# One last-row item of four transposed by the tensor engine instead of by VectorE and DRAM, with its product joined to its neighbour's

## The chip, the cores and the metric

The kernel runs on one core of one Trainium2 chip. The metric is the device time of one launch in microseconds (us); lower is better. The kernel before takes 1477.64 us (median of 3 runs, 1477.17 to 1479.41).

In the profile PE is the tensor engine's matmul, PEld its weight load, DVE is VectorE, ACT is ScalarE, POOL is GpSimd and SP is SyncE, which here only issues transfers (SPq is its queue). L727 is line 727 of the kernel before; a name such as `o` or `pt` is a tile.

## The reference

Attention that keeps the 32 largest scores of each row, then a layer with an exact GELU. All of it is float32.

```python
# q, k, v: (8, 8, 576, 64)
scores = np.matmul(q, k.transpose(0, 1, 3, 2)) / np.sqrt(64)
kth = np.partition(scores, -32, axis=-1)[..., -32:-31]
scores = np.where(scores >= kth, scores, -1e9)
attn = np.exp(scores - scores.max(-1, keepdims=True))
attn = attn / (attn.sum(-1, keepdims=True) + 1e-09)
x = np.matmul(attn, v)            # then (B, S, H*D): 4608 rows of 512
h = x @ w_in                      # 512 -> 2048
g = 0.5 * h * (1.0 + erf(h / np.sqrt(2)))
out = g @ w_out                   # 2048 -> 512
```

## The kernel before

**Items.** The attention is cut into 144 items of 128 rows of probabilities by twice 576 keys. A batch has eight heads, taken as four pairs, and 576 rows, that is four blocks of 128 and a last block of 64. An item of the first kind is one block of one pair, its two heads side by side. An item of the second kind, a last-row item, takes the 64 last rows of two pairs, that is of four heads. So a batch has 16 items of the first kind and 2 of the second. Batches go in twos, a ring of `RINGS` = 36 items: the even batch ends with its two last-row items (places 16 and 17 of the ring) and the odd batch starts with its own (places 18 and 19). These are the four last-row items of the title. There are four rings; in the first one these items are handled like the others, so the change bears on three: items 52 to 55, 88 to 91 and 124 to 127.

**Steps.** The kernel's order is written out by hand: a loop over steps n, each of which issues work of several items to all engines, in an order that every engine then keeps. In step n the scores of items n+2 and n+3 are multiplied (`scores`, at even n), DVE finds the 32 largest of item n (`top_k`), ACT makes the mask and the exponential of item n-1 (`softmax`), POOL sums, small statistics and the division (`threshold`, L516 and L517; `add_small`, L529; `normalise`, L571), and the probabilities of item n-2 are transposed. Between these, pieces of the layer with GELU (`mlp`: `h_ps`, `y_ps`, `seven`) are set, so that PE has work while the attention waits for the others.

**Two ways to transpose.** The product with v needs the probabilities transposed, in the tile `pt`, of which there is one buffer with room for two items (an even and an odd one). The odd items of the first kind, and everything up to item 26, go through PE: `transposes` gives one transpose of the tails (L647, together with the last keys' scores of item n+2, L371) and eight of 128 by 128 (L661); ACT copies them to `pt` (L650, L676). Items for which `squared` is true go another way: DVE transposes them in squares of 32 (`square_p`, L595, inside `top_k` of step n), SP writes them to DRAM in four transfers (`write_p`, L605, end of step n) and reads them back into `pt` in four (`read_p`, L615, in the next step). Even items of the first kind (but one per ring) and all last-row items behind item 26 are squared; the latter are called `delayed`.

**Products.** `attend(i)` multiplies with v into a PSUM tile `o` from `bank`, and ACT copies `o` to `xT` (L732, or L744 for a last-row item) when `copy_x` is called. From step 13 on `bank` has one buffer only, so that the next tile from it (`t_ps` or `tp_t` of L371, `seven`, `o`) waits until the copy before is done. For items of the first kind the product comes with the odd item. For last-row items: item 52 has its product at the start of step 56 (`even_last`), item 53 late in step 57, item 54 early and item 55 late in step 59 (`mid`, `mids`). The late ones are copied on ACT behind the first half of the softmax of item n-1. The same holds for 88 to 91 and 124 to 127, with 36 and 72 added.

**SP's queue.** SP issues in program order, and each issue waits for what it needs. Besides the writes and reads above it has the loads of q, k and v and the stores of y. When a last-row product of an even batch is done, the next batch's v is loaded for its two pairs, four transfers a pair (L138, L142). `issue` puts a load off to `flush`, behind the step's write, when the step has one (`held`); `issue_soon` runs those of `soon`, behind the step's read. Stores of y are collected and issued by `run_stores` at the end of the following step.

Of the kernel before, what the change touches and what calls it, by code (L numbers as in the profile page):

```python
# [14 lines left out]
def kernel(  # L15
# [78 lines left out]
            return raws[n][pair % 2 if pair < SQUARES else 0]  # L94
        return raws[n][pair % len(raws[n])]

    held, late_issues, soon = [False], [], []

    def issue_soon():
        while soon:  # L100
# [9 lines left out]
    def flush():  # L110
        held[0] = False
        while late_issues:
            late_issues.pop(0)()

    def load(n, pair, queue=None, queue2=None):
        if pair >= n_pairs:
# [161 lines left out]
    def bank(name):  # L278

        tag = "z" if few[0] else ("z", "y0", "y1", "y2")[turn[0] % 4]  # L280
        turn[0] += 1
        return ps.tile([P, 512], f32, tag=tag, bufs=1, name=name)
# [292 lines left out]
    def squared(i):  # L575

        if not SINGLE.stop - 2 < i < N - 2:
            return False
        return items[i][1] == NM or (i % 2 == 0 and i % RINGS != 12)

    def delayed(i):

# [117 lines left out]

    copies = []

    def column(tok):

        at = tok % RING
        return at if at < COLS else at - COLS

    def attend(i):

        if i < 0 or i >= N:  # L710
            return False
        pair, t = items[i]
        b, at = divmod(pair, NP)
        if t < NM and t % 2 == 0:
            return False
        pt = pt_now[0]
        o = bank("o")
        n, row = (2 * P, (t - 1) * P) if t < NM else (TL, SM)
        tok = place_of(b, row)
        gap = RING if t == NM else COLS if tok % RING >= COLS else RING - COLS  # L720
        assert read[0] >= tok - gap + n
        c = slice(column(tok), column(tok) + n)
        if t < NM:
            vt = raw_of("v", pair)
            for j in range(NJ):
                for e in range(2):
                    nc.tensor.matmul(  # L727
                        o[e * D : (e + 1) * D, 0:n], lhsT=vt[:, j, e, :],
                        rhs=pt[:, e * NJ + j if j < NM else NM, :],
                        start=(j == 0), stop=(j == NJ - 1),  # L730
                    )
            copies.append(lambda: nc.scalar.copy(out=xT[:, at, c], in_=o[:, 0:n]))  # L732
        else:
            for r in range(2):
                vt = raw_of("v", pair + r)
                for j in range(NJ):
                    for e in range(2):
                        nc.tensor.matmul(
                            o[e * D : (e + 1) * D, r * TL : (r + 1) * TL],
                            lhsT=vt[:, j, e, :],  # L740
                            rhs=pt[:, e * NJ + j if j < NM else NM, i % 2 * P :][:, half(r, e)],
                            start=(j == 0), stop=(j == NJ - 1),
                        )
            copies.append(lambda: nc.scalar.copy(  # L744
                out=xT[:, at : at + 2, c],
                in_=o[:, 0 : 2 * TL].rearrange("p (r n) -> p r n", n=TL),
            ))

        if t == (NM if b % 2 == 0 else NM - 1):
            for r in range(2 if t == NM else 1):  # L750
                f = lambda r=r: load("v", pair + r + NP)
                if r == 0 and delayed(i):
                    soon.append(f)
                else:
                    issue(f)
        if at == (NP - 1 if t < NM else NP - 2):
            assert n_tok[0] == tok
            n_tok[0] = tok + n
        return True
# [414 lines left out]
    for n in range(ahead):  # L1174

        held[0] = n < N and squared(n - 2)
        mid = [i for i in (n - 5, n - 4) if delayed(i) and n % 2 and (i % 2 or i in starts)]
        even_last = delayed(n - 4) and n % 2 == 0 and n - 4 not in starts
        if not mid and not even_last:
            read_p(n - 3)  # L1180

        def mids():
            attend(mid.pop(0))
            if not mid:
                copy_x()
                read_p(n - 3)
                issue_soon()
        left[0] = room_in(n)
        few[0] = n > START + 2
        eager[0] = n > N  # L1190
        left[0] += closes(n - 3) - closes(n - 2)
        if not waits(unit_in(n)):
            weights_add(unit_in(n))
        if n > 0:
            larger(n + 1)
        for piece in squares_in.pop(n, []):
            piece()
        if n == 1:

            for e in range(2):  # L1200
                select(0, e)
            for e in range(2):
                softmax(0, e)
        two = few[0] and n % 2 == 0 and n + 3 < N and items[n + 3][1] < NM
        scores(n + 2, two)
        if two:
            scores(n + 3)
        if even_last:
            product = attend(n - 4)
            issue_soon()  # L1210
            read_p(n - 3)
        else:
            product = not delayed(n - 3) and attend(n - 3)
        if len(mid) == 2:
            mids()
        late = n > START
        if n != 1 and n < START:

            for e in range(2):
                select(n - 1, e)  # L1220
            softmax(n - 1, 0)
        copy_x()
        if n == START:

            for e in range(2):
                select(n - 1, e)
            softmax(n - 1, 0)
        if waits(unit_in(n)):
            weights_size(unit_in(n))
            weights_add(unit_in(n))  # L1230
        mlp(1)
        if closes(n - 3):
            ready[0] = n_tok[0]
        if few[0] and n % 2:
            run_gelus()
        tr = transposes(n - 2)
        if product and n > START and done[0] < len(pieces) and pieces[done[0]][0] > ready[0]:

            for piece in tr[:1]:
                piece(n + 2 if few[0] else None)  # L1240
            tr, ready[0] = tr[1:], n_tok[0]
        if not few[0] and n > START:
            softmax(n - 1, 0)
        mlp(1)
        if n != 1 and not late:
            softmax(n - 1, 1)
        if few[0]:
            softmax(n - 1, 0)
            if n % 2:
                mlp(ODD)  # L1250
                if mid:
                    mids()
        mlp(1)
        prep = prep_in.pop(n, [])
        if n == 0:
            weights_size(unit_in(1))
            keep_busy(14, ident)
        if n == START + 1:

            for piece in prep:  # L1260
                piece(None)
            prep = []
        if len(prep) > 1 and len(tr) == 3:
            tr, prep = tr[:1] + prep[:1] + tr[1:], prep[1:]
        now = tr[:-1]
        if few[0]:
            now, tr, prep = tr + prep[:1], [], prep[1:]
        for x, piece in enumerate(now):
            piece(n + 2 if few[0] else None)
            ready[0] = n_tok[0]  # L1270
            if few[0] and x == 2:
                break
            mlp(1)
        ready[0] = n_tok[0]
        if late:
            softmax(n - 1, 1)
        if n > 0:
            smaller(n + 1)
        add_small(n - 1)
        for piece in tr[-1:] + prep:  # L1280
            piece(None)
            mlp(1)
        if n < START:

            keep_busy(4 if n == 0 else 8 if product else 14 if n < 5 else 18, ident)

        run_gelus()
        mlp(left[0])
        run_gelus()
        if n < N:  # L1290
            top_k(n, lambda: inverse(n - 1), lambda: square_p(n - 2))
            write_p(n - 2)
            flush()
            if n == 0:
                larger(1)
        else:
            inverse(n - 1)
        threshold(n)
        if n == 0:
            smaller(1)  # L1300
        normalise(n - 1)
        sum_up(n + 2)
        if n in sums_in:
            weight_sums(sums_in[n])
        run_small(6)

        if n > 0 and not waits(unit_in(n + 1)):
            weights_size(unit_in(n + 1))
        run_stores()
        if n == N:  # L1310
            run_stores()
        for m in (n + 1, n + 2):

            if m > 2 and waits(unit_in(m)) == (m == n + 1):
                load_weights(m)
        if n < NP:
            load("v", n)
        if n == 5:
            nc.vector.memset(flat["k"][0][TL:, 0:TL], 0.0)
            load("q", SQUARES)  # L1320
            load("k", SQUARES)
# [38 lines left out]
```

## Time and profile before

| | |
|---|---|
| runs | 1477.17, 1477.64, 1479.41 us |
| profiled execution, its own time | 1479.29 us |
| its span | 1477.5 us |
| PE busy | 98% of the span |
| DVE, POOL, ACT busy | 89%, 77%, 73% |
| mean granted clock of PE | 0.999 |
| transfers of `turned` and `pt` | 240 each way, 144 KB each |

The page shows one execution. Its busy shares are means over the whole kernel; a few microseconds have to be looked for in the waits of one engine and in the timelines of a stretch, which list instructions in the order of time: start, duration, engine, line, operation and tiles, how many were merged into the row, and in brackets the idle time before it and what ended it. A duration of PE has the time until the result is there, so that rows overlap; the time that an instruction takes from the next one is read from start to start.

### The profile page before, as it was taken

What the parts mean: (1) busy time and instruction counts of PE and PEld (TensorE: products, weight loads), DVE (VectorE), ACT (ScalarE), POOL (GpSimd) and SP (SyncE); (2) the same over time, 40 slices, a digit from 0 to 9 for tenths busy, and PEclk for the clock granted to TensorE, in tenths of its full rate; (3) what the DMA queues carried; (4) which work ended last, traced back from release to release, by engine and by line L of the source; (5) the groups of instructions that cost most, each with busy time, mean ns of one, the idle gap of its engine ahead of it and who ended that gap; (6) DMA issues with size and microseconds to landing.
All of it is one profiled execution on the core that took longest, in us unless ns stands there. A gap on an engine that the chain in (4) does not pass through costs nothing. (4 is left out here: it accounts for less than half of the span.)

```text
span 1477.5 us, 26521 instructions
## 1 busy us (share of the span) xinstructions
PE 1449.7 (98%) x8693; PEld 1134.6 (77%) x8693; DVE 1307.8 (89%) x3331; ACT 1082.8 (73%) x1902; POOL 1142.0 (77%) x1290
## 2 busy tenths in 40 slices
PE   8999999999999998999999999999999999999999
PEld 6776677887777776888777777787777777787787
DVE  7999899999999999899999999899999999898701
ACT  7999877877777686777777777677777777677620
POOL 6877567878898888777898978787788888887632
PEclk9999999999999999999999999999999999999999
DMA  7425210045435356345534347344543435523300
GB/s 198 144 86 129 78 47 1 24 92 103 93 71 91 67 107 129 65 95 112 102 81 78 74 74 151 76 92 96 99 101 73 89 63 97 125 61 73 68 15 15
DMA packets 544713, 127.04 MB, mean 86 GB/s; under 512 B 466464, under 2 KB 536128, under 8 KB 544576
## 3 DMA queue, kind: packets, MB, share of 16 engines
q1 hardware_dynamic: 543312, 124.93, 39.8%
q8 instruction: 69, 1.13, 0.3%
q14 instruction: 68, 0.56, 0.1%
q10 hardware_dynamic: 1200, 0.39, 0.1%
q0 software_dynamic: 64, 0.03, 0.0%
HBM read 80.47 MB, written 44.83 MB: 85 GB/s over the span
## 5 line engine op out<-in xcount | busy, mean ns | idle before, releaser
L790 PE MATMUL h_ps<-xT,w_in_sb 128*128 128x256 f32 (+1 forms) x2560 | 534.1, 361 | 0.0
L790 PEld LDWEIGHTS h_ps<-xT,w_in_sb 128*128 128x128 f32 x2560 | 437.5, 190 | 73.3 <-issue 25.2
L502 DVE MAX8 top<-lists 128x8 f32<-128x576 f32 (+1 forms) x792 | 475.5, 639 | 0.0
L505 DVE MATCH_REPLACE8 lists<-top,lists 128x288 f32<-128x288 f32 (+1 forms) x528 | 307.6, 588 | 0.0
L571 POOL TENSOR_TENSOR s<-s,stat 128x1152 f32<-128x1152 f32 x135 | 286.1, 2119 | 0.3 <-DVE stat L523 0.3
L536 ACT ACTIVATE s<-s,stat 128x576 f32<-128x576 f32 x288 | 224.7, 788 | 16.6 <-POOL stat L516 16.4
L548 ACT ACTIVATE s<-s,stat 128x576 f32<-128x576 f32 x288 | 224.6, 782 | 11.3 <-POOL lists L466 0.7
L529 POOL TENSOR_SCALAR stat<-stat 128x2 f32<-128x2 f32 x144 | 31.6, 219 | 210.4 <-ACT s L548 183.8
L474 POOL TENSOR_TENSOR lists<-lists 128x576 int32<-128x576 int32 x132 | 186.4, 1412 | 4.0
L466 POOL TENSOR_TENSOR lists<-s 128x576 int32<-128x576 int32 x133 | 188.0, 1413 | 0.0
L727 PE MATMUL o<-pt,raw_v 128*64 128x256 f32 x1280 | 152.9, 384 | 4.3 <-DMA pt<-turned 2.4
L806 ACT ACTIVATE g<-h_ps 128x512 f32<-128x512 f32 x144 | 78.2, 594 | 107.0 <-PE h_ps L790 106.8
L727 PEld LDWEIGHTS o<-pt,raw_v 128*64 128x64 f32 x1280 | 87.9, 136 | 88.3 <-issue 43.1
L946 PE MATMUL y_ps<-w_out_sb,sum 128*128 128x256 f32 x472 | 140.8, 380 | 0.0
L414 ACT ACTIVATE s<-s_ps 128x1024 f32<-128x1024 f32 x127 | 124.9, 1031 | 9.2 <-PE s_ps L406 8.8
L406 PE MATMUL s_ps<-kt,qm 64*128 64x512 f32 x512 | 129.4, 618 | 0.8 <-ACT s L412 0.8
L676 ACT COPY pt<-tp 128x1024 f32<-128x1024 f32 x73 | 74.4, 1019 | 56.2 <-PE tp L661 56.1
L505 DVE MATCH_REPLACE8 lists<-first,lists 128x288 f32<-128x288 f32 x264 | 114.2, 438 | 0.0
L946 PE MATMUL y_ps<-w_out_sb,g 128*128 128x256 f32 x480 | 113.4, 379 | 0.0
L523 DVE RECIPROCAL stat<-stat 128x2 f32<-128x2 f32 x144 | 22.9, 159 | 95.2 <-POOL stat L529 94.4
L502 DVE MAX8 first<-lists 128x8 f32<-128x288 f32 x268 | 106.5, 436 | 0.0
L441 DVE TENSOR_TENSOR lists<-s 128x576 f32<-128x576 f32 x133 | 101.1, 760 | 0.0
(162 smaller groups left out, 2483.3 us busy)
## 6 DMA issues: line engine op xcount, KB each, us to landing
turned<-s SPq DMA_DIRECT2D x240, 144.0 KB, 3.5
pt<-turned SPq DMA_DIRECT2D x240, 144.0 KB, 3.2
raw_v<-in_v_dram SPq DMA_DIRECT2D x64, 128.0 KB, 3.0
raw_q<-in_q_dram SPq DMA_DIRECT2D x112, 72.0 KB, 2.3
raw_k<-in_k_dram SPq DMA_DIRECT2D x112, 72.0 KB, 2.4
out_dram<-y SPq DMA_DIRECT2D x30, 256.0 KB, 2.1
w_out_sb<-in_moe_w_in_dram SPq DMA_DIRECT2D x14, 511.8 KB, 4.8
w_out_sb<-in_moe_w_out_dram SPq DMA_DIRECT2D x10, 511.8 KB, 4.1
```

Source lines behind the costliest of these rows:

```text
L406: nc.tensor.matmul(s_ps[:, e], lhsT=q_t[rows, :], rhs=kt[rows, main_keys(pair)], start=True, stop=True)
L414: nc.scalar.activation(spread(s, S + TL, SM), s_ps, func=AF.Copy, scale=scale)
L466: nc.gpsimd.tensor_tensor(t[:, :, 1].bitcast(i32), a.bitcast(i32), b.bitcast(i32), op=ALU.add)
L474: nc.gpsimd.tensor_tensor(into_of(i)[:, :, 1].bitcast(i32), both, top, op=ALU.subtract)
L502: nc.vector.max(x[:, e], src[:, e])
L505: nc.vector.match_replace(dst[:, e], x[:, e], src[:, e], LOWEST)
L536: nc.scalar.activation(s, s, func=AF.Prelu, bias=st["neg"][:, e : e + 1], scale=1.0, alpha=STEEP)
L548: nc.scalar.activation(s, s, func=AF.Exp, bias=st["bias"][:, e : e + 1], scale=1.0, accum_out=st["den"][:, e : e + 1],)
L571: nc.gpsimd.tensor_tensor(s, s, wide, op=ALU.mult)
L727: nc.tensor.matmul(o[e * D : (e + 1) * D, 0:n], lhsT=vt[:, j, e, :], rhs=pt[:, e * NJ + j if j < NM else NM, :], start=(j == 0), stop=(j = ...
L790: nc.tensor.matmul(h_tile(u)[:, i, :], lhsT=w_in_sb[:, ko, f * P : (f + 1) * P], rhs=xT[:, ko, c0 : c0 + n], start=(ko == 0), stop=(ko == ...
L946: nc.tensor.matmul(acc[names][:, k], lhsT=lhsT, rhs=rhs, start=(j == 0 and k == 0), stop=(j == FT // 2 - 1 and k == 1),)
```

## The change

In each of the three rings the second last-row item (53, 89, 125; place 17) is no longer squared. PE transposes it in step 55 and ACT copies it to `pt`, beside item 52's half, which is read from DRAM as before. Both products are then made in step 56, one right behind the other, in the two halves of one tile `o`, and one copy takes both to `xT`. The step that used to read item 53 and to multiply it does not do so any more. The loads of v that hang on these products are ordered anew: the first two pairs' right behind the joint product, the third's behind item 54's write, the fourth's behind item 55's write. The two stores of y that stood at the end of step 57 stand behind item 55's read at the start of step 58.

```diff
-    held, late_issues, soon = [False], [], []
+    held, late_issues, soon, later = [False], [], [], []
...
     def flush():
         held[0] = False
         while late_issues:
             late_issues.pop(0)()
+        late_issues.extend(later)
+        later.clear()
...
     def squared(i):
         if not SINGLE.stop - 2 < i < N - 2:
             return False
-        return items[i][1] == NM or (i % 2 == 0 and i % RINGS != 12)
+        if items[i][1] == NM:
+            return i % RINGS != RINGS // 2 - 1
+        return i % 2 == 0 and i % RINGS != 12
...
+    shared = []
...
     def attend(i):
...
-        o = bank("o")
+        both = t == NM and delayed(i - 1) and not delayed(i)
+        alone = t < NM or not delayed(i) or delayed(i ^ 1)
+        o = shared.pop() if both else bank("o")
+        off = 2 * TL if both else 0
...
-                            o[e * D : (e + 1) * D, r * TL : (r + 1) * TL],
+                            o[e * D : (e + 1) * D, off + r * TL : off + (r + 1) * TL],
...
-            copies.append(lambda: nc.scalar.copy(
-                out=xT[:, at : at + 2, c],
-                in_=o[:, 0 : 2 * TL].rearrange("p (r n) -> p r n", n=TL),
-            ))
+            if not alone:
+                shared.append(o)
+            else:
+                first = 0 if both else at
+                copies.append(lambda: nc.scalar.copy(
+                    out=xT[:, first : at + 2, c],
+                    in_=o[:, 0 : off + 2 * TL].rearrange("p (r n) -> p r n", n=TL),
+                ))
...
                 f = lambda r=r: load("v", pair + r + NP)
-                if r == 0 and delayed(i):
-                    soon.append(f)
+                if delayed(i):
+                    soon.insert(0, f)
+                elif both and r:
+                    later.append(f)
                 else:
                     issue(f)
...
+        def stores_later(m):
+            return m % 2 == 0 and delayed(m - 3) and m - 4 in starts
+
         even_last = delayed(n - 4) and n % 2 == 0 and n - 4 not in starts
-        if not mid and not even_last:
+        if not mid:
             read_p(n - 3)
+        if stores_later(n):
+            run_stores()
...
         if even_last:
             product = attend(n - 4)
+            attend(n - 3)
             issue_soon()
-            read_p(n - 3)
...
-        run_stores()
+        if not stores_later(n + 1):
+            run_stores()
```

## The prediction

> **What bounds the kernel now.** I read the page first, then the waits of the tensor engine (PE), then the timelines of each engine around the place that the change touches.
>
> ```profile
> span 1477.5 us, 26521 instructions
> ...
> PE 1449.7 (98%) x8693; PEld 1134.6 (77%) x8693; DVE 1307.8 (89%) x3331; ACT 1082.8 (73%) x1902; POOL 1142.0 (77%) x1290
> ```
>
> PE is idle for 27.8 us of 1477.5 only: the kernel is as long as PE's work plus its few waits. So an instruction added to PE costs its time in full, and a gain must come out of those 27.8 us. The waits of PE, longest first:
>
> ```profile
> PE o L738 <- DMA pt<-turned: 5.7, 3, 2.2
> ...
> PE o L727 <- DMA pt<-turned: 2.4, 2, 1.9
> PE t_ps L371 <- ACT xT L744: 2.2, 3, 0.7
> ```
>
> These 10.3 us all lie around the last-row items, in three places: items 52 to 55, 88 to 91 and 124 to 127 (rings 1, 2, 3 below). Ring 1 on PE, time of start and duration first, idle time and its releaser in brackets:
>
> ```profile
> 559.19 0.49 PE L371 MATMUL t_ps<-kt,qm 128*128 128x128 f32 x2 [0.74 <-ACT xT L744]
> ...
> 576.82 1.39 PE L738 MATMUL o<-pt,raw_v 128*64 128x64 f32 x40 [1.21 <-DMA pt<-turned]
> ...
> 579.41 0.49 PE L371 MATMUL tp_t<-kt,qm 128*128 128x128 f32 x2
> ...
> 587.31 2.38 PE L727 MATMUL o<-pt,raw_v 128*64 128x256 f32 x20 [1.91 <-DMA pt<-turned]
> ```
>
> 559.19 (step 57) stands behind item 53's product: the next user of that PSUM bank waits for its copy (0.74). 576.82 is item 55's product (step 59), late by its transposed rows. 587.31 (step 60) waits for item 56's. Rings 2 and 3:
>
> ```profile
> 926.13 1.39 PE L738 MATMUL o<-pt,raw_v 128*64 128x64 f32 x40 [2.25 <-DMA pt<-turned]
> ...
> 928.41 0.38 PE L371 MATMUL tp_t<-kt,qm 128*128 128x128 f32 x2
> 928.63 0.27 PE L647 MATMUL tp_t<-ident,s 128*128 128x128 f32 x1
> 928.74 0.60 PE L946 MATMUL y_ps<-w_sum,sum 128*128 128x256 f32 x2
> ...
> 929.61 1.04 PE L661 MATMUL tp<-ident,s 128*128 128x128 f32 x8
> 930.48 0.60 PE L946 MATMUL y_ps<-w_sum,g 128*128 128x256 f32 x2
> ...
> 934.81 2.38 PE L727 MATMUL o<-pt,raw_v 128*64 128x256 f32 x20 [0.52 <-DMA pt<-turned]
> ```
>
> ```profile
> 1273.51 2.12 PE L738 MATMUL o<-pt,raw_v 128*64 128x64 f32 x40 [2.20 <-DMA pt<-turned]
> ...
> 1277.37 0.39 PE L371 MATMUL tp_t<-kt,qm 128*128 128x128 f32 x2
> ...
> 1283.18 2.38 PE L727 MATMUL o<-pt,raw_v 128*64 128x256 f32 x20
> ```
>
> Ring 3 ran slower behind its wait: from product to L371 it took 3.86 us (1273.51 to 1277.37) against 2.28 in ring 2. In the first 2.1 us of it the granted clock, which stands behind the five engines' busy times, was 0.59:
>
> ```profile
> 1273.50:1275.60 2.10, 2.09 (x41) 1.98 (x41) 2.10 (x8) 1.39 (x3) 2.02 (x3) 0.59 0.93 143
> ```
>
> These 1.58 us belong to this execution: the profiled run took 1479.29 us, and without them 1477.71, which is the median shown (1477.64).
>
> **Added to PE.** Per ring, one tail transpose and eight more. From row to next row, L647 takes 0.11 us (928.63 to 928.74), the eight L661 0.87 (929.61 to 930.48): 0.98, on the path, 2.9 us in three rings. Merging two products into one run saves about two changes of tile shape, 0.1 us each at most; I count them as nothing.
>
> **Added to ACT, taken from DVE.** The two copies' groups, with busy time and mean ns:
>
> ```profile
> L676 ACT COPY pt<-tp 128x1024 f32<-128x1024 f32 x73 | 74.4, 1019 | 56.2 <-PE tp L661 56.1
> ...
> L650 ACT COPY pt<-tp_t 128x128 f32<-128x128 f32 x84 | 22.8, 271 | 3.0 <-PE tp_t L647 2.9
> ```
>
> ACT gets 1.02 + 0.27 = 1.29 us in step 55; the merge saves it one small copy in step 57, which I count as nothing. Behind the copies on ACT stands the exponential of item 54, and behind that POOL's small L529. What covers it:
>
> ```profile
> 543.85 0.22 POOL L529 TENSOR_SCALAR stat<-stat 128x2 f32<-128x2 f32 x1 [2.12 <-ACT s L548]
> 545.35 0.79 POOL L516 TENSOR_SCALAR stat<-top 128x2 f32<-128x2 f32 x1 [1.28 <-DMA turned<-s]
> ```
>
> Between L529 and L516 POOL idles 1.28 us. The row names a transfer, but L516 reads what DVE's top-k of item 55 leaves, so that is the real end, and from it the change takes a transpose of 1.36 us. So ACT's 1.1 to 1.3 us fill the gap that DVE leaves, and POOL goes on where it did, or 0.2 us earlier. I take 0.2; the bounds are 0 (ACT takes all) and 0.4. Without that cover each ring would lose up to 1.29 us.
>
> **Removed: the transfers.** Per ring four writes and four reads of SP vanish (item 53's), v's loads of the first two pairs go together behind the merged product, and the two stores of y step behind item 55's read. DVE's transposes of items 55 and 56 and SP in ring 1, then item 56's write and read in ring 2:
>
> ```profile
> 559.60 1.36 DVE L595 STREAM_TRANSPOSE s<-s 128x1152 f32<-128x1152 f32 x1
> ...
> 569.86 1.36 DVE L595 STREAM_TRANSPOSE s<-s 128x1152 f32<-128x1152 f32 x1
> ```
>
> ```profile
> 545.48 0.44 SPq L138 DMA_DIRECT2D raw_v<-in_v_dram  x1
> ...
> 548.41 2.57 SPq L615 DMA_DIRECT2D pt<-turned  x4
> ...
> 563.76 3.27 SPq L605 DMA_DIRECT2D turned<-s  x4
> ...
> 570.39 1.00 SPq L861 DMA_DIRECT2D out_dram<-y  x2
> 571.48 2.60 SPq L615 DMA_DIRECT2D pt<-turned  x4
> 574.19 3.39 SPq L605 DMA_DIRECT2D turned<-s  x4
> 581.88 2.54 SPq L615 DMA_DIRECT2D pt<-turned  x4
> ```
>
> ```profile
> 923.54 3.49 SPq L605 DMA_DIRECT2D turned<-s  x4
> ...
> 929.61 2.54 SPq L615 DMA_DIRECT2D pt<-turned  x4
> ```
>
> The rows from 563.76 on are item 55's write, the stores, 55's read, 56's write and read. A pair of v takes 2.9 us (545.48 to 548.41), a write 3.3, a read 2.6; from a write to the read that needs it 6.1 us (ring 2) to 7.7 (ring 1). With the change v's two pairs run from about 546.5 (1 us later than now, for PE's transposes) to 552.4, 54's write to 555.7, one more pair to 558.6, 54's read starts at 558.6 to 560.1. So 55's write starts between 561.2 (DVE done at 560.96) and 562.7 instead of 563.76, its read 6.1 to 7.7 later, 567.3 to 570.4, instead of 571.48. From that read to PE's product it was 5.3 us (to 576.82), so the rows are there at 572.6 to 575.7; PE comes at 576.82 - 1.21, or 0.2 later with what follows: 575.8. The DMA wait is gone. 56's write then starts between 571.3 (DVE done at 571.2) and 574.1, now 574.19, and its product is free to start that much earlier than 587.31: between 584.4 and 587.2. I take 585.4. In rings 2 and 3, with the 6.1, it is well clear.
>
> **Where the stall goes.** Both DMA waits and the L371 wait gone, less the transposes, would be 3.86 - 0.98 in ring 1 (and PE would be 0.98 - 0.74 = 0.2 late at item 55's product, as used above). But in step 59 a second thing ends just behind the DMA: the copy of item 55's product, which stands on ACT behind the first half of item 58's softmax:
>
> ```profile
> 576.20 0.78 ACT L536 ACTIVATE s<-s,stat 128x576 f32<-128x576 f32 x1 [1.24 <-POOL stat L516]
> ...
> 579.11 0.25 ACT L744 COPY xT<-o 128x128 f32<-128x128 f32 x1
> ```
>
> ```profile
> 924.47 0.77 ACT L536 ACTIVATE s<-s,stat 128x576 f32<-128x576 f32 x1 [1.24 <-POOL stat L516]
> ```
>
> ```profile
> 1271.90 0.78 ACT L536 ACTIVATE s<-s,stat 128x576 f32<-128x576 f32 x1 [1.25 <-POOL stat L516]
> ```
>
> L536 waits for item 58's threshold, that is for DVE and POOL, not for PE. From L536 the copy comes at +2.91 and L371, which needs the bank, at +3.21 (576.20 to 579.41). PE, early by then, is there at 575.8 + 2.28 = 578.1 and will stand at L371 for about 1.1 us. So L371 starts at L536 + 3.21 less the 0.2: 579.21, 927.48 and 1274.91, against 579.41, 928.41 and 1277.37. From L371 to L727 is 5.81 us without a wait (ring 3), 5.9 behind a stall (0.49 for 0.38 above), so PE is at L727 at 585.1, 933.4, 1280.8; with the transfer ring 1 starts at 585.4. That is 1.9, 1.4 and 2.4 us earlier. Behind L727 the rings ran alike whatever stood before, so it stays. PE's 2.9 us lie within the new wait and are paid already.
>
> **Sum.** 5.7 us off the profiled run: 1479.29 - 5.7 = 1473.6. To the median: ring 3's 1.58 us of low clock are mostly not in it; ring 3's gain then is 0.8, or 1.3 if a wait like ring 2's 0.52 stands there instead. 1477.64 - (1.9 + 1.4 + 0.8 to 1.3) = 1473.0 to 1473.5. I say 1473.2.
>
> One rule is weighed here. The row: after 2.20 us of waiting the clock fell to 0.59 and cost 1.58 us, while after 2.25, 1.91 and 1.21 us it cost nothing. The Trainium skill (TensorE: Matmul & The Clock Gate, Part 1) has the clock fall only after an idle window of about 3.4 us; by that rule a 1.1 us wait is free, and the sum stands. The trace disagrees once in four.
>
> **The rivals.**
> PE is held by nothing (0.15): POOL's chain comes over 1.1 us earlier since DVE has less to do, and L371 doesn't wait. Then ring 1 gains 3.86 - 0.98 = 2.9, ring 2 0.74 + 2.25 + 0.52 - 0.98 = 2.5, ring 3 at least 2.0: 1470.2. Against it: POOL's L529 at 543.85 waits for ACT, which gets later.
> The clock falls behind the new waits (0.13): up to 1.58 us a ring; one drop gives 1474.8, two 1476.4.
> The transfers stay late (0.11): v's loads in one run hold 54's write, and what L371 gains is waited away at L727 in all rings: 1476.5 to 1477.6.
> ACT becomes the bound (0.08), the slower case. In step 55 its big copy would wait for PE's transposes, as it does in step 59:
>
> ```profile
> 581.78 1.01 ACT L676 COPY pt<-tp 128x1024 f32<-128x1024 f32 x1 [1.18 <-PE tp L661]
> ```
>
> Then 1.29 + 1.18 = 2.47 us go into item 54's exponential, and if POOL's gap at 545.35 doesn't take them (its end being something else than DVE's top-k), L536 of step 59 comes 2.47 later. L727 then starts at 576.20 + 2.47 + 3.21 + 5.9 = 587.8 in ring 1, 0.5 late; in ring 2 at 936.1, 1.2 late; in ring 3, against 1281.6 without the low clock, at 1283.5, 1.9 late: 1477.64 + 3.6 = 1481.2. It turns to a loss once the delay passes about 1.3 us. Against it: ACT lies behind PE in step 55 (no idle before its copies there), so the transposes should be ready when it comes.
> The order doesn't change as said (0.01): 1477.6.
>
> **How the numbers follow.** The forecast has 0.52, with a range of its own of 1471.7 to 1475.1 (cover 0 to 0.4 in each ring, ring 1's transfer from 584.4 to 587.2). 0.2% is 2.95 us, about what a measurement of this kernel can tell: faster is below 1474.7. From the forecast 0.48, from the free PE 0.15, from the clock 0.07: faster 0.70. Same: 0.04, 0.06, 0.11 and 0.01, 0.22. Slower 0.08. The range for 8 in 10, from the free PE to the late transfers' better end: 1469.6 to 1476.6.
>
> **What would show it.** Right: no wait for pt's DMA at L738 and L727 in rings 1 to 3; a wait of L371 for xT's copy in step 59, 0.6 to 1.8 us in each ring; POOL's L516 of step 55 within 0.4 us of its old place after the row before; DVE's transposes 57 instead of 60; L661 24 more. Wrong: L371 in step 59 without a wait (then faster than said), L676 in step 55 behind a PE wait, or DMA waits of pt left at L727.

## The result, and the profile after

The changed kernel takes 1473.85 us (median of 8 runs, 1473.37 to 1474.59), the kernel before beside it 1478.04 us (8 runs, 1477.17 to 1479.56): a ratio of 0.997 with a 95% interval of 0.9959 to 0.9981, 4.2 us or 0.28% faster. The prediction was 1473.2 us, and 0.2% as the bound of what can be told.

| | before | after |
|---|---|---|
| profiled execution, its own time | 1479.29 us | 1473.45 us |
| its span | 1477.5 us | 1471.4 us |
| ring 1: start of item 56's product (L727, now L736) | 587.31 | 585.04 |
| ring 2 | 934.81 | 931.05 |
| ring 3 | 1283.18 | 1277.07 |

The lines have moved: L371 is L373 now, L516 L518, L529 L531, L536 L538, L595 L599, L605 L609, L615 L619, L647 L651, L650 L654, L661 L665, L676 L680, L727 L736, L738 L747, L744 L757, L861 L876.

The busy time of each engine on the page of the changed kernel:

```profile
PE 1450.0 (99%) x8720; PEld 1136.2 (77%) x8720; DVE 1304.3 (89%) x3328; ACT 1084.8 (74%) x1905; POOL 1141.0 (78%) x1290
```

PE has as much to do as before (1449.7), in a span that is 6.1 us shorter. What went is waiting. The longest of PE's waits after, in total, number and longest one:

```profile
PE tp_t L373 <- ACT xT L757: 4.7, 3, 1.6
```

No wait for a transfer of `pt` is left. Instead of 10.3 us in three kinds there are 4.7 in one, the one that was foretold. Ring 1 on PE after, with start, duration, and in brackets the idle time before:

```profile
539.86 0.38 PE L373 MATMUL tp_t<-kt,qm 128*128 128x128 f32 x2
540.08 0.27 PE L651 MATMUL tp_t<-ident,s 128*128 128x128 f32 x1
540.19 0.60 PE L961 MATMUL y_ps<-w_sum,sum 128*128 128x256 f32 x2
...
541.05 1.04 PE L665 MATMUL tp<-ident,s 128*128 128x128 f32 x8
541.93 0.60 PE L961 MATMUL y_ps<-w_sum,g 128*128 128x256 f32 x2
...
545.67 2.55 PE L747 MATMUL o<-pt,raw_v 128*64 128x64 f32 x80
548.15 2.86 PE L805 MATMUL h_ps<-xT,w_in_sb 128*128 128x256 f32 x12
...
575.09 1.39 PE L747 MATMUL o<-pt,raw_v 128*64 128x64 f32 x40
...
579.13 0.49 PE L373 MATMUL tp_t<-kt,qm 128*128 128x128 f32 x2 [1.59 <-ACT xT L757]
...
585.04 2.38 PE L736 MATMUL o<-pt,raw_v 128*64 128x256 f32 x20
```

The added transposes are there, L651 and eight L665; the joint product is one run of 80 (545.67); item 55's product (575.09) and item 56's (585.04) wait for nothing. Only L373 waits, for the copy of item 55's product. In rings 2 and 3 it is the same:

```profile
925.14 0.49 PE L373 MATMUL tp_t<-kt,qm 128*128 128x128 f32 x2 [1.57 <-ACT xT L757]
...
1271.16 0.49 PE L373 MATMUL tp_t<-kt,qm 128*128 128x128 f32 x2 [1.57 <-ACT xT L757]
```

The three waits are equal within 0.02 us, which transfers never were (2.25, 2.20, 1.21 before). What a ring gains itself is what its L736 is earlier by, less what the rings ahead had gained: 587.31 - 585.04 = 2.27 in ring 1, of which 0.08 was there at its start (539.94 against 539.86); 3.76 in ring 2 less the 2.33 that its own step 55 comes earlier by, 1.43; 6.11 less 3.72 in ring 3, 2.39.

### The profile page after: what moved, and what is told of

Its sections match the earlier page's. It is cut to its first block, busy times and chain, and to the rows that moved or that the text cites. A ratio compares the mean times of both kernels' runs of the same rounds, so it can differ in the third digit from the quotient of the medians.

```text
span 1471.4 us, 26527 instructions
## 1 busy us (share of the span) xinstructions
PE 1450.0 (99%) x8720; PEld 1136.2 (77%) x8720; DVE 1304.3 (89%) x3328; ACT 1084.8 (74%) x1905; POOL 1141.0 (78%) x1290
## 5 line engine op out<-in xcount | busy, mean ns | idle before, releaser
L538 ACT ACTIVATE s<-s,stat 128x576 f32<-128x576 f32 x288 | 225.3, 791 | 13.4 <-POOL stat L518 13.3
L550 ACT ACTIVATE s<-s,stat 128x576 f32<-128x576 f32 x288 | 225.3, 786 | 11.3 <-POOL lists L468 0.7
L531 POOL TENSOR_SCALAR stat<-stat 128x2 f32<-128x2 f32 x144 | 31.4, 218 | 208.7 <-ACT s L550 194.6
L736 PE MATMUL o<-pt,raw_v 128*64 128x256 f32 x1280 | 153.0, 384 | 1.8 <-ACT s L550 1.2
L736 PEld LDWEIGHTS o<-pt,raw_v 128*64 128x64 f32 x1280 | 87.4, 136 | 86.1 <-issue 43.2
L680 ACT COPY pt<-tp 128x1024 f32<-128x1024 f32 x76 | 77.5, 1020 | 56.2 <-PE tp L665 56.1
```

Of the source, the lines that this page charges most:

```text
L538: nc.scalar.activation(s, s, func=AF.Prelu, bias=st["neg"][:, e : e + 1], scale=1.0, alpha=STEEP)
L550: nc.scalar.activation(s, s, func=AF.Exp, bias=st["bias"][:, e : e + 1], scale=1.0, accum_out=st["den"][:, e : e + 1],)
L736: nc.tensor.matmul(o[e * D : (e + 1) * D, 0:n], lhsT=vt[:, j, e, :], rhs=pt[:, e * NJ + j if j < NM else NM, :], start=(j == 0), stop=(j = ...
```

## The experiments

All edits are to the changed kernel unless said. The times in the table are medians, with the kernel before on the same chip beside it.

| run | us | before | ratio, 95% interval |
|---|---|---|---|
| e1 stores alone (edit to the kernel before) | 1478.91 | 1478.80 | 1.0003, 0.9994 to 1.0012 |
| e2 stores early | 1473.63 | 1478.80 | 0.9965, 0.9953 to 0.9978 |
| e3 loads unsorted | 1484.59 | 1478.80 | 1.0038, 1.0026 to 1.0051 |
| e4 copy first | 1472.56 | 1478.80 | 0.9956, 0.9944 to 0.9969 |
| e5 product twice | 1475.50 | 1479.30 | 0.9973, 0.9961 to 0.9985 |
| e6 copy twice | 1477.54 | 1479.30 | 0.9986, 0.9977 to 0.9995 |
| e7 product apart | 1478.50 | 1479.30 | 0.9995, 0.9985 to 1.0005 |
| e8 copy first, stores last | 1471.31 | 1479.30 | 0.9938, 0.9926 to 0.9951 |
| e9 the changed kernel again | 1474.16 | 1478.35 | 0.9972, 0.9961 to 0.9983 |
| e10 item 54's product twice | 1474.78 | 1478.35 | 0.9976, 0.9967 to 0.9985 |
| e11 copy first, again | 1472.10 | 1478.35 | 0.9956, 0.9943 to 0.9968 |
| e12 copy first, stores last, again | 1470.57 | 1478.35 | 0.9947, 0.9934 to 0.9959 |

### One part alone: the stores (e1, e2)

In e1 the kernel before gets only the move of the stores behind item 55's read; in e2 the changed kernel loses it.

```diff
+        if stores_later(n):
+            run_stores()
...
-        run_stores()
+        if not stores_later(n + 1):
+            run_stores()
```

> The kernel before with one part of the change alone: the two stores of y step behind item 55's read. My theory (PE is held in step 59 first by item 55's read, then by the copy of its product on ACT, and in step 60 by item 56's transfer): item 55's read comes about 1.1 us earlier, so the wait of PE at its product falls to about 0.1 us in ring 1 and 1.1 us in rings 2 and 3; L371 behind it starts no earlier than 3.2 us after ACT's L536, and item 56's write and read keep their place, because SP has as much to do ahead of them. So L727 keeps its place in ring 1 and 2 and little is won: 0 to 1.5 us faster than before. Rival (the stores were the cause of the waits at the products): 1.1 us in each ring and what hangs on it, 3 us or more faster.

> The changed kernel without the moved stores: they stand at the end of step 57 again, ahead of item 55's read. My theory: the read comes 1.1 to 1.3 us later, near 568.7 in ring 1, its rows are there near 574, still ahead of PE at 575.1, and PE has another 1.57 us to spare at L373 of step 59; item 56's write keeps its place. No change against the changed kernel: 4.2 us faster than before, within 0.6. Rival (the order of the stores is what removed the waits): 3 us or more of the gain go.

e1 leaves the time where it was. Ring 1 on PE in e1:

```profile
576.15 1.39 PE L738 MATMUL o<-pt,raw_v 128*64 128x64 f32 x40
...
580.01 0.49 PE L371 MATMUL tp_t<-kt,qm 128*128 128x128 f32 x2 [1.42 <-ACT xT L744]
...
588.29 2.38 PE L727 MATMUL o<-pt,raw_v 128*64 128x256 f32 x20 [2.29 <-DMA pt<-turned]
```

The wait of 1.21 us for item 55's rows is gone, and nothing is won: 1.42 us are waited at L371 for the copy instead, and L727 waits 2.29 for item 56's rows where it waited 1.91. In rings 2 and 3 the product still waits (0.61 and 0.69 us), then L371 (0.75 and 0.68) and L727 (1.75 and 1.08). Ring 1 shows the new bound most plainly: whoever takes away the transfer alone meets the copy 3 us later, and the next transfer behind it. e2 has the same 4.7 us at L373 as the changed kernel, and its time is 0.2 us off (1473.63 against 1473.85); by the kernel before beside it, it gained 5.2 us where 4.2 within 0.6 was said, but the two times of the kernel before differ by more than that (1478.80 and 1478.04). The stores' move is worth nothing that can be measured in either kernel.

### The order of v's loads (e3)

```diff
-                if delayed(i):
-                    soon.insert(0, f)
-                elif both and r:
-                    later.append(f)
+                if r == 0 and delayed(i):
+                    soon.append(f)
                 else:
                     issue(f)
```

> The changed kernel with the loads of v in the rule of before: only the first pair's right behind the product, the three others' behind item 54's write. My theory: three loads of 2.75 us each stand ahead of item 54's read, so SP is some 4 to 5 us later with item 55's write and read; the read starts near 572, PE waits 1 to 2.5 us at item 55's product, which costs nothing or up to 1 us because it would have stood at L373 for 1.57 us anyway; but item 56's write and read come 4 us later too, and PE waits for them at L736 (1.5 to 3 us a ring). So 4 to 8 us slower than the changed kernel, that is as long as before or up to 4 us longer. Rival (SP has time enough once item 53's eight transfers are gone): within 1 us of the changed kernel.

The direction was right, the size larger than said: 11 us slower than the changed kernel (e2 beside it), 5.8 slower than before. SP's queue in ring 1, first of the changed kernel, then of e3:

```profile
551.02 3.94 SPq L609 DMA_DIRECT2D turned<-s  x4
...
557.88 2.58 SPq L619 DMA_DIRECT2D pt<-turned  x4
...
567.43 2.58 SPq L619 DMA_DIRECT2D pt<-turned  x4
...
571.49 4.57 SPq L609 DMA_DIRECT2D turned<-s  x4
578.88 2.54 SPq L619 DMA_DIRECT2D pt<-turned  x4
```

```profile
562.65 2.87 SPq L619 DMA_DIRECT2D pt<-turned  x4
...
572.43 2.54 SPq L619 DMA_DIRECT2D pt<-turned  x4
...
584.27 1.89 SPq L619 DMA_DIRECT2D pt<-turned  x3
```

With three pairs of v between item 54's write and its read, that read starts 4.8 us later (562.65 against 557.88), and the reads behind it are 5.0 and 5.4 us late. PE's waits in e3:

```profile
PE o L736 <- DMA pt<-turned: 7.1, 3, 3.1
PE o L747 <- DMA pt<-turned: 5.0, 3, 2.4
```

These 12.1 us, less the 4.4 that L373 waits less (4.7 against 0.3), are 7.7 of the 11.4 us by which the span grew (1482.8 against 1471.4). The rest lies in the clock. The stretches behind the waits in e3 (sum and busy time of PE, PEld, DVE, ACT and POOL, then the granted clock, DMA's share and GB/s):

```profile
577.60:579.70 2.10, 2.05 (x41) 1.96 (x41) 2.10 (x8) 1.45 (x3) 2.02 (x3) 0.63 0.93 178
579.70:581.50 1.80, 1.80 (x5) 1.44 (x6) 1.80 (x6) 0.27 (x1) 1.40 (x1) 0.50 0.77 122
...
1286.80:1290.10 3.30, 3.30 (x21) 2.02 (x21) 3.30 (x6) 0.01 (x1) 3.22 (x5) 0.70 0.13 21
1290.10:1294.00 3.90, 3.90 (x16) 3.38 (x17) 2.25 (x5) 2.06 (x5) 2.14 (x3) 0.82 0.86 133
```

Length times what the clock lacks: 0.78 + 0.90 + 0.99 + 0.70 = 3.4 us. With the waits that makes 11.1 of 11.4. A further drop in e3, from 69.3 to 73 us, lies far ahead of the change and is made up for by ring 1: v's first load starts there at 546.50, in the changed kernel at 546.38.

### Is PE's own work the bound? (e5, e10)

Two kernels give PE 1.31 us more a ring: e5 makes item 53's product twice, e10 item 54's.

```diff
-            for r in range(2):
+            for r in (0, 1, 0, 1) if both else range(2):
```

```diff
-            for r in range(2):
+            for r in (0, 1, 0, 1) if b % 2 and i % 2 == 0 and delayed(i) else range(2):
```

> The changed kernel with item 53's product made twice into the same place (40 more rows on PE in step 56 of each ring, 1.31 us of PE, 3.9 us in all). My theory: PE has 1.57 us to spare in step 59, where L373 waits for a copy that stands behind a softmax on ACT, and that softmax hangs on DVE and POOL and not on PE; so the wait falls to about 0.3 us and the time stays that of the changed kernel, within 0.6 us (1473.7). Rival (PE is the bound in these steps as well, and each microsecond added to it shows): 3.9 us slower than the changed kernel.

> Item 54's product (90's, 126's) is made twice on PE, 1.31 us more work a ring, at a place where no load of v hangs on it and between the transposes and the wait of step 59. Theory (the copy of item 55's product on ACT sets L373, PE waits there 1.59 us): L373 stays where it is, its wait falls to about 0.3 us, L736 does not move, time within 0.5 us of the changed kernel. Rival (PE's own work sets the time, or work behind the product is held up): 3 x 1.31 = 3.9 us slower than the changed kernel.

At L373 both do what the theory says. e5, then e10, ring 1 on PE:

```profile
579.07 0.49 PE L373 MATMUL tp_t<-kt,qm 128*128 128x128 f32 x2 [0.41 <-ACT xT L757]
```

```profile
579.59 0.49 PE L373 MATMUL tp_t<-kt,qm 128*128 128x128 f32 x2 [0.44 <-ACT xT L757]
...
585.50 2.38 PE L736 MATMUL o<-pt,raw_v 128*64 128x256 f32 x20
```

In e5 the wait shrinks from 1.59 to 0.41 us and L373 stays where it was, 579.07 against 579.13. In e10 the whole execution had come to this place 0.44 us later (the joint product started at 546.11, in the changed kernel at 545.67); less that, L373 and L736 are at 579.15 and 585.06, against 579.13 and 585.04. In rings 2 and 3 of e10, counted from the joint product, L373 keeps its place too (0.03 and 0.02 us later), but L736 does not: it waits 0.45 and 0.93 us for item 56's rows. In ring 2 this lateness is older than the added work. Item 55's write took 4.68 us on SP (at 907.82), in the changed kernel 3.32 (at 907.36), and item 55's read started at 915.35, ahead of the doubled product (916.86). That is one execution, and the slowest of e10's eleven (1478.55): it also has a wait of 2.25 us for `pt` at 1392.97, far behind the change, with a clock of 0.50 to 0.65 for 4 us behind it.

In the median the 3.9 us of added work cost 0.6 us (1474.78 against 1474.16 in e9), a sixth, just past the bound of 0.5; the two intervals overlap. e5 took 1.65 us more than the changed kernel, past the 0.6 that was said, though by the kernel before beside each it is 0.4 (3.80 us gained against 4.19). In its trace L736 waits 1.25 and 0.51 us for item 56's rows in rings 2 and 3. The loads of v overwrite what e5's product reads, and item 54's write comes 0.5 us later in ring 1 (551.54 against 551.02); but e10, on whose product no load hangs, has the same waits, so that the loads cause them is not shown. What is shown is that PE's work does not set L373: in all three rings of both kernels it takes 1.31 us more and L373 stays.

### Is the cover on ACT used up? (e6)

ACT's large copy of item 53 is made twice.

```diff
+            for _ in range(2 if items[i][1] == NM and SINGLE.stop - 2 < i < N - 2 else 1):
                 nc.scalar.copy(
```

> The changed kernel with ACT's large copy of item 53 to pt made twice in step 55 (one more copy of 1.02 us a ring, 0.91 from start to start, ahead of item 54's exponential). My theory: POOL's L531 of step 55 waits for that exponential, and POOL has no pause from there to step 58, so DVE, POOL and the copy of step 59 all come 0.9 us later, the wait at L373 rises from 1.57 to about 2.4 us, and the kernel is 2.7 us slower than the changed one (1476.4). Rival (ACT is busy 74% of the span and has room for it): no change.

POOL in ring 1, first of the changed kernel, then of e6:

```profile
544.85 0.22 POOL L531 TENSOR_SCALAR stat<-stat 128x2 f32<-128x2 f32 x1 [3.21 <-ACT s L550]
545.15 0.22 POOL L518 TENSOR_SCALAR stat<-top 128x2 f32<-128x2 f32 x1
...
575.10 0.79 POOL L518 TENSOR_SCALAR stat<-top 128x2 f32<-128x2 f32 x1 [0.56 <-DVE stat L525]
```

```profile
545.76 0.22 POOL L531 TENSOR_SCALAR stat<-stat 128x2 f32<-128x2 f32 x1 [4.23 <-ACT s L550]
...
576.00 0.79 POOL L518 TENSOR_SCALAR stat<-top 128x2 f32<-128x2 f32 x1 [0.57 <-DVE stat L525]
```

In the changed kernel POOL goes from L531 to L518 at once; the gap of 1.28 us that stood there is full. So a second copy delays POOL by 0.91 us, and 30 us later item 58's threshold is still 0.90 late, and L373 with it (580.02 against 579.13). The wait at L373 did not grow to 2.4 us as said, only to 1.67: PE comes later too, because at L960 it waits 2.0 us in all for POOL's `g`.

The time rises by 2.4 us (1.76 gained against the kernel before, the changed kernel 4.19) to 3.7 (the medians themselves); 3 x 0.9 = 2.7 was expected. Part of this spread is the clock. Behind the wait in ring 3 the granted clock was 0.64, 0.50 and 0.83 (1274.5 to 1276, to 1278, to 1279), and from L373 to item 56's product it took 7.59 us; in ring 2, behind a wait of the same length, 5.91 (927.51 to 933.42). Ring 3 on PE in e6:

```profile
1274.55 0.49 PE L373 MATMUL tp_t<-kt,qm 128*128 128x128 f32 x2 [1.67 <-ACT xT L758]
...
1282.14 2.38 PE L737 MATMUL o<-pt,raw_v 128*64 128x256 f32 x20
```

These 1.68 us belong to the profiled execution (1478.67). Of e6's eleven times five lie from 1476.1 to 1476.9, about 2.7 us above the changed kernel, and five from 1478.4 to 1479.1; that the clock makes the difference is shown for the profiled execution only. The mechanism of the prediction's rival, ACT as the bound, is real, and it begins where the change stops.

### The product apart (e7)

Item 53 is still transposed by PE, but its product is made in step 57, as before, and the two pairs' loads hang on it there (`lone` is true for items 53, 89 and 125).

```diff
-        both = t == NM and delayed(i - 1) and not delayed(i)
-        alone = t < NM or not delayed(i) or delayed(i ^ 1)
+        both, alone = False, True
...
-                elif both and r:
-                    later.append(f)
+                elif lone(i) and r == 0:
+                    soon.append(f)
...
-        mid = [i for i in (n - 5, n - 4) if delayed(i) and n % 2 and (i % 2 or i in starts)]
+        mid = [i for i in (n - 5, n - 4) if (delayed(i) or lone(i)) and n % 2 and (i % 2 or i in starts)]
...
-            attend(n - 3)
```

> The changed kernel with item 53's product made apart, late in step 57 as in the kernel before, in a tile and a copy of its own; v's loads for its two pairs follow it, one behind item 54's read and one behind item 55's write. My theory: the wait of L373 in step 57 (0.74 us) is back but lies within the 1.57 us to spare in step 59; what costs is that the third pair's load now stands between item 54's read and item 55's write, so that 55's read and 56's write and read come some 3 us later and PE waits for 56's rows at L736: 2 to 4.5 us slower than the changed kernel. Rival (joining saves PE's wait and nothing else): no change, or 0.74 us a ring, 2.2 us, if PE's spare time doesn't hold it.

Nothing that can be measured is left of the gain (0.9995, interval 0.9985 to 1.0005). By the kernel before beside each, e7 is 3.4 us slower than the changed kernel, within the 2 to 4.5 that were said. SP's queue, then PE, in ring 1 of e7, whose lines stand two or three further on:

```profile
561.12 0.60 SPq L140 DMA_DIRECT2D raw_v<-in_v_dram  x1
...
563.60 3.37 SPq L612 DMA_DIRECT2D turned<-s  x4
...
582.06 2.54 SPq L622 DMA_DIRECT2D pt<-turned  x4
```

```profile
587.31 2.38 PE L738 MATMUL o<-pt,raw_v 128*64 128x256 f32 x20 [2.05 <-DMA pt<-turned]
```

A pair of v stands ahead of item 55's write again (561.12), the write starts at 563.60, where it started before the change (563.76), item 56's read at 582.06 (before 581.88), and item 56's product at 587.31, where it was. One thing came out otherwise: L373 in step 57 (559.38) does not wait for the copy of item 53's product, so its 0.74 us are not what joining pays with. The eight transfers less do not pay by themselves. The early, joint product lets v's loads go early, out of the way of the write of item 55; e7 moves the product and the loads together, but e3, which moves the loads alone, loses the gain as well.

### What comes next (e4, e8, e9, e11, e12)

If the copy on ACT is the bound, then issuing it ahead of the softmax half must gain. e8 and e12 put the stores behind item 56's write besides; e9 is the changed kernel, e11 and e12 are e4 and e8 again, on one chip.

```diff
-            softmax(n - 1, 0)
+            ahead_of = n % 2 and len(mid) > 0
+            if not ahead_of:
+                softmax(n - 1, 0)
...
                     mids()
+            if ahead_of:
+                softmax(n - 1, 0)
```

> The changed kernel with one thing moved: in step 59 ACT copies item 55's product ahead of the first half of item 58's softmax instead of behind it. My theory: the 1.57 us wait of L373 for this copy vanishes in all three rings, PE comes 1.5 us earlier to L736 and there stands 0.7 to 1.0 us for item 56's read (which starts at 578.9, 925.1 and 1271.2, and needs some 5.3 us to the product): 0.5 to 0.9 us a ring are left, 2 us faster than the changed kernel in all (1 to 4.5). Rival (the wait is set by PE's or POOL's own work and the copy only happens to end last; ACT's softmax, 0.8 us later, then delays POOL and DVE): no gain, or up to 2.4 us slower.

> The kernel with the copy of step 59 ahead of the softmax half, and the two stores of y now behind item 56's write too. My theory: of the 1.57 us that the earlier copy frees, 0.7 to 1.35 us were given back at L736, which waits for item 56's rows; SP starts that write 0.5 us (ring 1) to 2 us (rings 2 and 3) earlier without the stores ahead of it, so 0.5 to 1.3 us a ring of this wait go: 1.5 to 3 us faster than with the copy alone, 1469.5 to 1471. Rival (the write's four transfers land late because the DMA engines are busy, not because they are issued late): no change.

> The changed kernel itself, on the chip of the three runs beside it, so that they can be set against it directly. Expected 1473.6 to 1474.2 us, with a wait of about 1.6 us of L373 for the copy of xT in step 59 of each ring.

> The copy of item 55's product stands ahead of the softmax half on ACT, once more, beside the changed kernel itself. Theory: 1.0 to 1.5 us faster than the changed kernel, the rest of its 4.7 us of wait being taken by item 56's rows and POOL's division. Rival (the earlier difference came from the run): within 0.5 us of it.

> The same, and the stores of y behind item 56's write. Theory (the wait for item 56's rows is what the copy's gain went into, and SP's queue sets it): 2.2 to 3.5 us faster than the changed kernel, 1 to 2 faster than the copy alone. Rival: within 0.5 us of the copy alone.

Side by side: 1474.16 (e9), 1472.10 (e11), 1470.57 us (e12). The copy's order gains 2.1 us (1.1 in e4 against e2), the stores another 1.5. PE's waits in e4:

```profile
PE tp_t L651 <- POOL s L573: 3.0, 7, 0.5
...
PE o L736 <- DMA pt<-turned: 2.7, 2, 1.4
```

L373's 4.7 us are gone, and 2.7 of them are back at L736, which now waits for item 56's rows, and 1.4 more at L651 (3.0 against 1.6), which waits for POOL's division. This execution was the slowest of e4's five (1473.92); in e11's, which took the median of 1472.10, only 1.3 us are back at L736. SP's queue, then PE, in ring 1 of e12:

```profile
578.28 2.54 SPq L619 DMA_DIRECT2D pt<-turned  x4
```

```profile
578.25 0.33 PE L651 MATMUL tp_t<-ident,s 128*128 128x128 f32 x1 [0.42 <-POOL s L573]
...
583.89 2.38 PE L736 MATMUL o<-pt,raw_v 128*64 128x256 f32 x20
```

Item 56's rows are read at 578.28 instead of 578.88, and its product starts at 583.89 without a wait. What is left at the place is 0.42 us a ring, and 0.20 at L736 in ring 3. This kernel beats both: 0.9947 (0.9934 to 0.9959) of the kernel before, and 0.9938 in e8. e11 gained more than was said of it (2.1 us for 1.0 to 1.5), e12 stands 3.6 us ahead of e9 (2.2 to 3.5 said) and 1.5 ahead of e11 (1 to 2 said), and e8 fell a little short.

## Why the prediction was right

**The bound.** "A gain must come out of those 27.8 us": PE's work is 1450.0 us after and 1449.7 before, and the span went from 1477.5 to 1471.4. "An instruction added to PE costs its time in full" is too broad, as the prediction's own sum has it: where a later wait takes it up, most of it is free (0.6 of 3.9 us in e10).

**Transposes on PE, 0.98 us a ring, paid in the new wait.** From row to row after: 0.11 (540.08 to 540.19) and 0.88 (541.05 to 541.93), 0.99. The counts are as said: 624 of L665 for 600 of L661, and 57 transposes on DVE for 60. That added work goes into the wait there, e10 shows: 1.31 us a ring leave L373 in its place in all three rings.

**The merge, counted as nothing.** This term was mis-sized: PE comes to item 55's product at 575.09, not at 575.8. Rows of the kernel before, around the second product:

```profile
554.18 1.89 PE L946 MATMUL y_ps<-w_out_sb,g 128*128 128x256 f32 x8
556.00 1.39 PE L738 MATMUL o<-pt,raw_v 128*64 128x64 f32 x40
557.31 0.70 PE L946 MATMUL y_ps<-w_sum,sum 128*128 128x256 f32 x2
557.85 0.59 PE L946 MATMUL y_ps<-w_out_sb,sum 128*128 128x256 f32 x2
```

and of the changed kernel, where that product is missing:

```profile
556.25 1.89 PE L961 MATMUL y_ps<-w_out_sb,g 128*128 128x256 f32 x8
557.97 0.59 PE L961 MATMUL y_ps<-w_sum,sum 128*128 128x256 f32 x2
558.40 0.59 PE L961 MATMUL y_ps<-w_out_sb,sum 128*128 128x256 f32 x2
558.84 0.38 PE L373 MATMUL t_ps<-kt,qm 128*128 128x128 f32 x2
```

The same layer rows take 1.82 + 0.54 + 0.60 us beside a product (the last one to 559.19 less its wait of 0.74) and 1.72 + 0.43 + 0.44 without: 0.37. The joint product takes 2.48 (545.67 to 548.15) where two take 2 x 1.31 (556.00 to 557.31): 0.14. L371 behind its stall cost 0.10. Together 0.6 us a ring. It made the new wait longer: 1.59 where "about 1.1" was said, inside the 0.6 to 1.8. It did not change the time, since L373 starts when the copy lets it.

**ACT's copies in the gap that DVE leaves.** L518 starts at 545.15 for 545.35, and item 58's L538 at 575.92 for 576.20: 0.28 us earlier, of which 0.08 was there at the ring's start, so 0.2 as was taken. The large copy did not wait for PE's transposes (542.13, no idle before it). e6 shows that this cover has no more room.

**The transfers.** Item 55's read was to start at 567.3 to 570.4 and started at 567.43; item 56's write at 571.3 to 574.1 and started at 571.49. Ahead of them SP was faster than any bound: 54's read started at 557.88 (558.6 to 560.1 said), 55's write at 560.74 (561.2 to 562.7). The term that was too large is v's: two pairs behind each other took 4.64 us (546.38 to 551.02), not 2 x 2.9. The choice of 585.4 for item 56's product, out of 584.4 to 587.2, was 0.3 us too late or more: PE came at 585.04 and didn't wait.

**The new bound.** L371 was put at 579.21, 3.21 behind L536. ACT after, ring 1:

```profile
575.92 0.78 ACT L538 ACTIVATE s<-s,stat 128x576 f32<-128x576 f32 x1 [1.41 <-POOL stat L518]
...
578.83 0.24 ACT L757 COPY xT<-o 128x128 f32<-128x128 f32 x1
```

575.92 + 3.21 = 579.13, where L373 stands. The copy comes 2.91 us behind L538, as before; 1.28 of them are a load of ACT's table (`ACT_TABLE_LOAD`, L550, at 576.76) ahead of the exponential, which the prediction did not take apart and no run here takes out. e4 and e11, which issue the copy ahead of all this, take the wait away.

**The sum.** 1.9, 1.4 and 2.4 us were said for the three rings, 2.19, 1.43 and 2.39 came; the 0.3 of ring 1 is the transfer's bound. The profiled executions differ by 5.84 us (5.7 said), the medians by 4.2 (4.1 to 4.6 said). The difference of the two is about the 1.58 us of low clock, which the profiled execution of before had and that of the changed kernel had not. Of the 0.65 us between 1473.2 and 1473.85, 0.40 come from the kernel before, which took 1478.04 us here instead of 1477.64. The forecast's own range, 1471.7 to 1475.1, does not quite follow from its bounds: cover of 0 to 0.4 in each ring and ring 1's transfer up to 587.2 give 1472.1 to 1475.7. The time lies in both.

**The rivals.** PE held by nothing: not so, it waits 4.7 us. The clock behind the new waits: no drop behind the 1.57 to 1.59 us of the changed kernel, and none of its 8 times, of e2's 5 or of e9's 7 lies more than 0.8 us above its median. But one of the three waits of 1.67 us in e6 had one. So this rival is not shown to be far off, and the mis-sized merge, which made the wait 0.5 us longer than said, brought it nearer; that it stayed away is in part luck. The late transfers: not here, but it is what e3 and e7 show as soon as the loads stand otherwise, and dearer than said. ACT as the bound: in step 55 ACT's exponential already is what POOL's L531 waits for, and L518 goes right behind it, only no later than DVE had set it before; the margin is nearly nothing.

## What to carry to other kernels

A wait that is removed is worth the distance to what ends second at that place, so look for the copy that has to free the PSUM bank and for what it stands behind on its engine; here that order alone held 1 to 2 us. In a queue that issues in order, the loads that stand between a write and its read decide more than the number of transfers: the changed kernel with its loads unsorted makes fewer transfers than the kernel before and is 5.8 us slower. And work that goes to another engine is free only as far as the gap that it fills, which can be read beforehand (1.28 us here) and is used up afterwards.

## What was not expected of the hardware

The granted clock fell behind waits of PE of 2.20 us (before, ring 3), 2.36 and 3.09 us (e3), 1.67 us (e6, ring 3) and 2.25 us (e10, at 1392.97), to 0.50 to 0.83 for about 4 to 7 us, and once behind 1.30 us (e3, at 69.36; 0.50 from 70 to 72). It did not fall behind 2.25 us (before, ring 2), 2.29 (e1), 2.14 (e3), 2.05 (e7), the 1.67 of e6's other two rings or the 1.57 to 1.59 of the changed kernel. So the length of the wait does not decide by itself, and these rows show no length from 1.3 us on that is safe. The Trainium skill (TensorE: Matmul & The Clock Gate, Part 1) puts it at an idle window of about 3.4 us; by the rows here that is too long, and the measurement decides. One drop cost 1.58 us (before) and 1.68 (e6), and in e3 the two behind the moved loads were worth 3.4 of 11.4 us, so such a wait can cost more than its length.
